# Two-chunk attention blocks from chunk 8 on, each behind an output projection

## The chip, the cores and the metric

One core of a Trainium2 chip runs the kernel. The metric is the time of one execution on the device, in microseconds, as the median of several runs. A profile of one execution gives the trace that is read below; engines are TensorE (PE, with its weight loads as PEld), VectorE (DVE), ScalarE (ACT), GpSimd (POOL) and SyncE (SP).

## What is computed

Sliding-window causal attention, then a SwiGLU feed-forward block on its output. Inputs are float32, and so is the output of 4608 x 512.

```
batch, n_heads, seq, head_dim = 8, 8, 576, 64;  window = 64
scores = (q @ k^T) / sqrt(64);  kept where 0 <= query - key < 64
attn_out = softmax(scores) @ v
x = attn_out.transpose(0, 2, 1, 3).reshape(4608, 512)
g = x @ w_gate                      # 512 x 1536
out = (g * sigmoid(g) * (x @ w_val)) @ w_out    # 1536 x 512
```

## The kernel before

The 4608 tokens are 36 chunks of 128. Four chunks make one FFN chunk c of 512 tokens (nine of them). All matmuls are bf16.

**Attention of a chunk n.** K and Q come from DRAM by DMAs that POOL issues (load, with a cast to bf16), then are transposed: chunks 0 to 9 two at a time by TensorE (T2, 16 transposes on tiles of 128x64, copied out by ACT), chunks 10 on by DMA transposes that SP issues in program order (T; Tkq is k and q). Scores are S(n) (Sa, Sb and the mask multiplication Sm on DVE) or, from chunk KC = 18 on, Sk(n), which lays keys out differently and has 16 matmuls where Sb has 24. Scores need the transposed k and q of their chunk and, in Sb, k of the chunk before, in Sk, q of the chunk after. ACT takes the exponentials into pt. The product with V is AVmm (32 matmuls on 64x64 tiles, in two phases), or AVs (16 matmuls on 128x64 tiles, for which vs holds V shifted by 64 rows; only chunks 0 to 3 use it). A column of ones in V yields the sums, and AVn (AVpn for two chunks) divides on DVE into xb. X(n) transposes xb into xT: by a DMA transpose on SP, or by four TensorE transposes with a copy on ACT or DVE.

**Blocks.** B(n) is AVmm phase 0 of chunk n, the scores of chunk n+1, AVmm phase 1, AVn. P(n) is the same for two chunks n and n+1: AVp phase 0, Sk(n+2), Sk(n+3), AVp phase 1, AVpn. P uses PSUM banks 0 to 6. B runs for chunks 4, 6 and 8 to 15, P from chunk P0 = 16 on.

**FFN.** F(c, fs, lo, hi) computes slices of 128 of the 1536 hidden columns for tokens lo to hi of chunk c: four matmuls for the gate, four for the value (per slice), tanh on ACT, two multiplications on DVE into hT. One slice on 512 tokens or two slices on 256 fill a PSUM bank each. O(c, u) is the output of 128 tokens: 12 matmuls over hT and Wo, a copy on ACT and a store.

**Order.** build() writes the whole order by hand up to chunk 11, and a loop over c = 2 to 8 and u = 0 to 3 the rest, with n = 4c + u + 4. Each operation goes to its engine's queue in that order; semaphores come from the reads and writes that an operation names. At most 16 DMAs of POOL, 16 of SP and 8 of ACT are under way. PSUM banks are taken from two lists, "f" for F, O and X, "a" for attention, which banks() replaces at given points. Buffers that a later load waits for: eight each for k and q of a chunk, ten for V.

Of the kernel before, what the change touches and what calls it, by code (L numbers as in the profile page):

```python
# [7 lines left out]
B, H, S, D = 8, 8, 576, 64  # L8
DM, DFF = H * D, 1536
T = B * S  # L10
NCH = T // 128
NFC = T // 512
NF = DFF // 128
# [139 lines left out]
class _Kernel:  # L153
# [7 lines left out]
    NO = 4  # L161
    NST = 4
    KC = 18
    P0 = 16

    def __init__(self, nc, q, k, v, wg, wv, wo, out):
        self.nc, self.q, self.k, self.v = nc, q, k, v
# [203 lines left out]
    def kt(self, n):  # L371
        return n + 3 + (n >= 13)

    def qt(self, n):
        return n + 3 + (n >= 12) + (n >= 15)
# [103 lines left out]
    def S(self, n, bias=False):  # L479
        if n < NCH:  # L480
            self.Sb(self.Sa(n, bias))
# [43 lines left out]
    def shift(self, n, r, eng):  # L525
        i = n + r - 1
        src, dst = self.va[n], self.vs[i]
        rows = slice(64 * r, 64 * r + 64)
        rd = [("va", n), ("va", n, 0), ("va", n, 1)] + (["mask"] if eng == "pool" else [])
        self.copy(eng, dst[rows, :, 0:64], src[rows, :, 0:64], rd, [("vs", i, r)])  # L530

    def AVs(self, st):
        n, bx, av, done = st
        va, pt = self.va[n], self.pt[n % self.NP]
        vs = self.vs[n - 1] if n else va

        def pe(e):
            for j in range(4):
                for p in range(2):
                    h = 2 * j + p  # L540
                    for c, vv in ((0, vs), (1, va)):
                        x = e.matmul(av[64 * c:64 * c + 64, p, j, :], pt[:, h, 64 * c:64 * c + 64], vv[:, h, 0:65],
                                     start=j == 0, stop=True, skip_group_check=True)
            return x

        ip = n % self.NP
        rd = [("pt", ip, 0), ("pt", ip, 1), ("va", n), ("va", n, 0), ("va", n, 1)]
        if n:
            rd += [("vs", n - 1, 0), ("vs", n - 1, 1)]
        done.append(self.g.op("pe", pe, reads=rd, writes=[b[1] for b in bx]))  # L550

    def AVn(self, st):
# [69 lines left out]
    def P(self, n):  # L622
        bx = [self.bank("a") for _ in range(3)]
        d = self.AVp(n, 0, bx, None)
        for m in (n + 2, n + 3):
            if m < NCH:
                self.Sk(m)
        self.AVp(n, 1, bx, d)
        self.AVpn(n, bx)

    def AV(self, n):
        st = self.AVa(n)
        self.AVmm(st, 0)
        self.AVmm(st, 1)
        self.AVn(st)
# [14 lines left out]
    def X(self, n, eng="sp", kind="f"):  # L650
        if n >= NCH:
            return
        g = self.g
        ix, it, u = n % 4, (n // 4) % self.NX, n % 4
        xb = self.xb[ix]
        xo = self.xT[it][:, :, 128 * u:128 * u + 128]
        xk = [("xb", ix, 0), ("xb", ix, 1)]
        if eng == "sp":
            g.op("sp", lambda e: e.dma_start_transpose(xo, xb[:, :]), reads=xk, writes=[("xT", it, u)], dma=True)
            return  # L660
        bank, bk = self.bank(kind)
        tb = bank[:, 0:256].bitcast(BF).rearrange("p (c t) -> p c t", c=4)

        def pe(e):
            for c in range(4):
                r = e.transpose(tb[:, c, :], xb[:, 128 * c:128 * c + 128], self.ident[:, :])
# [75 lines left out]
    def hTk(self, ih):  # L742
        return [("hT", ih, f) for f in range(NF)]

    def O(self, c, u):
        g = self.g
        ih = c % self.NH
        hT = self.hT[ih]
        io = (4 * c + u) % self.NO
        ost = self.ost[io]  # L750
        OB, ok = self.bank("f")

        def pe(e):
            for f in range(NF):
                r = e.matmul(OB[:, :], hT[:, f, 128 * u:128 * u + 128], self.Wo[:, f, :],  # L755
                             start=(f == 0), stop=(f == NF - 1))
            return r

        g.op("pe", pe, reads=self.hTk(ih) + [("Wo", f) for f in range(NF)], writes=[ok])
# [71 lines left out]
    def late_loads(self):  # L831
        self.load2(4, "k")
        self.load2(4, "q")
        self.load_wo(0, 6)
        self.load_wo(6, 12)
        self.load(10, "kq")
        self.load(8, "v")
        self.load(11, "kq")
        self.load(9, "v")

    def Tkq(self, n):
        self.T(n, "k")
        self.T(n, "q")

    def build(self):
        F, S, AV, X, T2, O = self.F, self.S, self.AV, self.X, self.T2, self.O
        self.loads()
        self.banks("a", [4, 5, 6, 7, 0, 1, 2, 3, 4, 5, 0, 1, 2, 3, 4, 5, 6, 7, 0, 1, 2, 3, 4, 5, 6, 7, 6, 7])
        self.warm(44, n=132)
        self.first_T(("dve", "act"))  # L850
        s0 = self.Sa(0)
        T2(0, "q", ("act", "dve"))
# [101 lines left out]
        lk, lq = 15, 15  # L954
        tk, tq = 14, 14
        for c in range(2, NFC):
            for u in range(4):
                n = 4 * c + u + 4
                if n == self.P0:
                    self.banks("f", [self.bank("f")[1][1], self.bank("f")[1][1], 5, 6, 7] + [7, 3, 4, 5, 6, 0, 1, 2, 7, 3, 4, 5, 6, 7] * 11)  # L960
                    self.banks("a", [0, 1, 2, 3, 4, 5, 6])
                if n == NCH:
                    self.banks("f", [3, 4, 5, 6, 0, 1, 2, 7])
                if n < NCH:
                    while lk < self.kt(n + 1):
                        lk += 1
                        self.load(lk, "k")
                    while lq < self.qt(n + 1):
# [3 lines left out]
                if n == 15:  # L972
                    self.init_kmask()
                if n < self.P0:
                    self.B(n)
                    self.X(n)
                if n < NCH:
                    while tk < self.kt(n):
                        tk += 1
                        self.T(tk, "k")  # L980
                    while tq < self.qt(n):
# [6 lines left out]
                if n == self.P0 - 1:  # L988
                    if n + 2 >= self.KC:
                        self.Sk(n + 2)  # L990
                        self.Sm(n + 2)
                    else:
                        S(n + 2)
# [5 lines left out]
                if self.P0 <= n < NCH - 2:  # L999
                    self.Sm(n + 2)  # L1000
                if n >= NCH and u == 3:
                    O(c - 1, u)
# [46 lines left out]
```

## Time and profile before

| | us |
|---|---|
| median of 3 runs | 331.41 |
| lowest, highest | 330.72, 331.79 |
| profiled execution | 330.58 |
| its span, first to last instruction | 328.8 |
| TensorE busy | 321.9 |
| VectorE busy | 202.0 |
| ScalarE busy | 136.8 |
| GpSimd busy | 107.0 |

In a row of the timeline stand the start, the time from the first start to the last end of merged instructions, engine and line, operation, tiles out<-in, the tile shape on the array, the shape of the data and the count; in brackets the idle time before and what ended it. Matmuls overlap, so that the next start tells more than the length. A row of one tile's instructions ends with their first and last start; "DMA to landing" is the time from the issue of a DMA to its last write. In a row of groups, busy time and mean ns follow the count. The clock granted to TensorE was 1.000 of full speed on average.

### The profile page before, as it was taken

The page shows a single profiled execution, that of the slowest core. Times are in us where ns is not written, and L with a number is a line of the kernel's source. Part 1 is how long each engine was busy: PE and PEld are TensorE (multiplying, and loading weights), DVE is VectorE, ACT ScalarE, POOL GpSimd, SP SyncE. Part 2 cuts the span into 40 slices and gives each one's busy share as a digit, 9 for nine tenths or more (in the row PEclk, how much of TensorE's full clock was granted, in tenths as well). Part 3 has the DMA queues.
Part 4 walks back from the last instruction along what each step waited for, and adds up shares of the span by engine and source line. Part 5 has one row for each costly group of instructions (what it writes and reads, how often), then busy time and mean ns, then how long its engine had stood idle before and what let it go on. Part 6 is the DMA issues. An engine that isn't in the chain of part 4 may idle for free.

```text
span 328.8 us, 8102 instructions
## 1 busy us (share of the span) xinstructions
PE 321.9 (98%) x3463; PEld 167.9 (51%) x3463; DVE 202.0 (61%) x350; ACT 136.8 (42%) x244; POOL 107.0 (33%) x137
## 2 busy tenths in 40 slices
PE   7999999999999999999999999999999999999997
PEld 6585576656444445454545454545454544444443
DVE  4676874675666657576666656565656566555520
ACT  2645665554334535252525252525243432332222
POOL 8999977544534444155151220100000000000000
PEclk9999999999999999999999999999999999999999
DMA  9999999999999999999999975562422111300012
GB/s 145 178 192 186 176 201 156 152 154 152 174 176 175 157 171 162 174 155 154 132 129 117 126 87 106 83 99 58 105 57 57 50 50 50 48 32 33 34 57 102
DMA packets 157892, 39.47 MB, mean 120 GB/s; under 512 B 144928, under 2 KB 153376, under 8 KB 157856
## 3 DMA queue, kind: packets, MB, share of 16 engines
q0 software_dynamic: 109008, 18.62, 74.6%
q1 hardware_dynamic: 43392, 10.82, 23.5%
q10 hardware_dynamic: 5456, 9.51, 8.9%
q8 instruction: 27, 0.44, 0.6%
q14 instruction: 9, 0.07, 0.1%
HBM read 37.75 MB, written 9.44 MB: 144 GB/s over the span
## 4 chain that ended last, share of the span: by engine, by line
PE 90%; POOL 4%; DMA 3%; ACT 1%; DVE 1%; issue 1%; ACTq 0%; POOLq 0%
PE ps L729 55%; PE ps L755 27%; DMA xT<-xb 3%; PE ps L590 2%; PE ps L514 1%; POOL va L314 1%; PE ps L457 1%; POOL vs L243 1%; PE ps L777 1%; PE ps L363 1%; POOL Wg L329 1%; POOL qs L323 1%; PE ps L421 0%; PE ps L425 0%; POOL Wv L329 0%
## 5 line engine op out<-in xcount | busy, mean ns | idle before, releaser
L737 DVE SCALAR_TENSOR_TENSOR uu<-sig,ps 128x512 bf16<-128x512 bf16 x108 | 73.9, 684 | 66.7 <-ACT sig L735 66.5
L729 PE MATMUL ps<-xT,Wg 128*128 128x512 bf16 (+1 forms) x480 | 111.3, 359 | 1.1 <-DMA xT<-xb 0.9
L729 PE MATMUL ps<-xT,Wv 128*128 128x512 bf16 (+1 forms) x480 | 111.1, 358 | 0.0
L755 PE MATMUL ps<-Wo,hT 128*128 128x512 bf16 x420 | 95.9, 380 | 0.0
L735 ACT ACTIVATE sig<-ps 128x512 bf16<-128x512 f32 x108 | 64.9, 600 | 70.9 <-PE ps L729 70.7
L739 DVE SCALAR_TENSOR_TENSOR hT<-uu,ps 128x512 bf16<-128x512 bf16 x108 | 74.2, 687 | 3.7
L729 PEld LDWEIGHTS ps<-xT,Wv 128*128 128x128 bf16 x480 | 46.9, 98 | 46.5
L729 PEld LDWEIGHTS ps<-xT,Wg 128*128 128x128 bf16 x480 | 44.5, 98 | 44.0 <-issue 1.6
L755 PEld LDWEIGHTS ps<-Wo,hT 128*128 128x128 bf16 x420 | 40.8, 98 | 49.0
L760 ACT ACTIVATE ost<-ps 128x512 f32<-128x512 f32 x35 | 20.9, 597 | 93.3 <-PE ps L755 93.3
L314 POOL DMA_DIRECT2D va<-in_v_dram x40 | 34.9, 883 | 32.6 <-PE ps L590 28.3
L314 POOL DMA_DIRECT2D kn<-in_k_dram x29 | 25.0, 867 | 36.6 <-DMA kT<-kn 29.6
L314 POOL DMA_DIRECT2D qn<-in_q_dram x29 | 24.9, 868 | 31.4 <-DMA qT<-qn 23.1
L433 ACT ACTIVATE pt<-ps 128x512 bf16<-128x512 f32 x36 | 19.4, 596 | 9.6 <-PE ps L425 9.2
L469 ACT ACTIVATE pt<-ps 128x512 bf16<-128x512 f32 x36 | 18.6, 603 | 3.7 <-PE ps L461 3.7
L617 DVE RECIPROCAL rp<-ps 128x14 f32<-128x14 f32 (+1 forms) x20 | 4.1, 204 | 25.6 <-PE ps L590 25.6
L477 DVE TENSOR_TENSOR pt<-pt,mask 128x1024 bf16<-128x1024 bf16 x14 | 9.6, 684 | 8.2 <-ACT pt L433 8.2
L619 DVE TENSOR_TENSOR xb<-ps,rp 128x896 bf16<-128x896 f32 (+1 forms) x20 | 13.8, 692 | 0.7
L477 DVE TENSOR_TENSOR pt<-pt,kmask 128x1024 bf16<-128x1024 bf16 x18 | 12.3, 685 | 0.0
L561 DVE TENSOR_TENSOR xb<-ps,rc 128x512 bf16<-128x512 f32 x16 | 11.1, 692 | 0.6
L590 PEld LDWEIGHTS ps<-va,pt 64*64 64x64 bf16 x632 | 7.7, 107 | 4.4 <-issue 4.2
L590 PE MATMUL ps<-va,pt 64*64 64x65 bf16 x632 | 9.5, 194 | 0.1
(64 smaller groups left out, 153.3 us busy)
## 6 DMA issues: line engine op xcount, KB each, us to landing
out_dram<-ost ACTq DMA_DIRECT2D x35, 256.0 KB, 3.3
va<-in_v_dram POOLq DMA_DIRECT2D x32, 128.0 KB, 10.8
kn<-in_k_dram POOLq DMA_DIRECT2D x23, 128.0 KB, 16.7
qn<-in_q_dram POOLq DMA_DIRECT2D x23, 128.0 KB, 16.6
Wg<-in_moe_w_gate_dram POOLq DMA_DIRECT2D x6, 256.0 KB, 7.4
Wv<-in_moe_w_val_dram POOLq DMA_DIRECT2D x6, 256.0 KB, 7.1
Wo<-in_moe_w_out_dram POOLq DMA_DIRECT2D x2, 768.0 KB, 14.5
qs<-in_q_dram POOLq DMA_DIRECT2D x3, 256.0 KB, 6.5
```

The costliest lines, as they stand in the source:

```text
L314: self.g.op("pool", lambda e, d=d, a=a: e.dma_start(d, a), writes=ks, dma=True)
L433: g.op("act", lambda e, po=po, p=p: e.activation(po, sv[p], ACTF.Exp, scale=SCALE), reads=[bx[p][1]], writes=[pk[p]])
L469: g.op("act", lambda e, po=po, p=p: e.activation(po, sv[p], ACTF.Exp, scale=SCALE), reads=[bx[p][1]], writes=[pk[p]])
L477: self.g.op("dve", lambda e: e.tensor_tensor(pt, pt, m, ALU.mult), reads=pk + [key], writes=pk)
L590: z = e.matmul(self.psa[64 * c:64 * c + 64, o:o + 65], pt[p][rows, h, 64 * a:64 * a + 64], va[m][rows, h, 0:65], start=first, stop=phase = ...
L619: g.op("dve", lambda e, d=d, num=num, rb=rb: e.tensor_tensor(d, num, rb, ALU.mult), reads=bk + [("rp", k)], writes=xk)
L729: r = e.matmul(bank[:, a * n:a * n + n], W[:, kk, f * 128:f * 128 + 128], xT[:, kk, lo:hi], start=(kk == 0), stop=(kk == NK - 1))
L735: g.op("act", lambda e, G=bank: e.activation(sig[:, 0:w], G[:, 0:w], ACTF.Tanh, scale=0.5), reads=[bk], writes=[("sig", i)])
L737: g.op("dve", lambda e: e.scalar_tensor_tensor(uu[:, 0:w], sig[:, 0:w], 1.0, G[:, 0:w], ALU.add, ALU.mult), reads=[("sig", i), gk], writes ...
L739: g.op("dve", lambda e: e.scalar_tensor_tensor(out, v3(uu), 0.5, v3(V), ALU.mult, ALU.mult), reads=[("uu", i), vk], writes=[("hT", ih, f) ...
L755: r = e.matmul(OB[:, :], hT[:, f, 128 * u:128 * u + 128], self.Wo[:, f, :], start=(f == 0), stop=(f == NF - 1))
L760: g.op("act", lambda e: e.activation(ost[:, :], OB[:, :], ACTF.Copy), reads=[ok], writes=[("ost", io)])
```

## The change

- Chunks 8 to 15 are done by P, two at a time, and no longer by B. P computes scores by Sb for chunks below 18. For n = 8 and 10 the second AV phase comes between the two scores. S(8) and S(9) run together ahead. Each of P(8), P(10), P(12), P(14) and P(16) follows an output O at once.
- AV of chunks 5 and 7 uses AVs; POOL makes the shifted copies in four more instructions, between loads (shift with a given buffer).
- FFN slices 6 and 7 of c = 1 are each done once on 512 tokens, not as a pair on two halves.
- x of chunk 10 is transposed by TensorE with a copy on ACT; that of chunk 7 is put between the halves of O(0,1) and copied by DVE.
- O(0,0) comes before AV of chunk 7, O(2,0) before c = 3, O(2,1) before P(16); the order of loads and transposes up to chunk 21 is written out, and the key mask is made earlier. P(16) and later blocks are as before.
- The warm-up matmuls are 48 of 121 columns, not 44 of 132.

```diff
+    def shift(self, n, r, eng, i=None):
+        i = n + r - 1 if i is None else i
...
     def AVs(self, st):
-        vs = self.vs[n - 1] if n else va
+        iv = n - 1 if n < 4 else (7 - n) // 2
+        vs = self.vs[iv] if n else va
...
     def P(self, n):
         for m in (n + 2, n + 3):
-            if m < NCH:
+            if m < self.KC:
+                self.Sb(self.Sa(m), False)
+            elif m < NCH:
                 self.Sk(m)
-        self.AVp(n, 1, bx, d)
+            if (m == n + 2) == (n < 12):
+                self.AVp(n, 1, bx, d)
         self.AVpn(n, bx)
...
-    def O(self, c, u):
+    def O(self, c, u, mid=None):
+        parts = ((0, NF),) if mid is None else ((0, NF // 2), (NF // 2, NF))
...
     def late_loads(self):
         self.load_wo(6, 12)
+        self.shift(4, 1, "pool", 1)
+        self.shift(5, 0, "pool", 1)
         self.load(10, "kq")
...
         self.load(9, "v")
+        self.shift(6, 1, "pool", 0)
+        self.shift(7, 0, "pool", 0)
...
-        self.warm(44, n=132)
+        self.warm(48, n=121)
...
-        AV(5)
+        a5 = self.AVa(5)
+        self.AVs(a5)
+        self.AVn(a5)
...
         F(1, (4, 5), 0, 256)
         X(6, "act")
         T2(4, "k", ("act", "act"))
-        F(1, (6, 7), 0, 256)
+        O(0, 0)
         a7 = self.AVa(7)
-        self.AVmm(a7, 0)
+        self.AVs(a7)
         T2(4, "q", ("act", "act"))
-        self.AVmm(a7, 1)
         self.AVn(a7)
         self.load(12, "kq")
         self.load(10, "v")
         for n in range(10, 12):
             self.Tkq(n)
-        O(0, 0)
-        X(7, "act")
+        O(0, 1, lambda: X(7, "dve"))
         self.load(13, "kq")
         self.load(11, "v")
         S(8)
-        O(0, 1)
+        S(9)
+        (new list of "f" banks)
+        F(1, (6,))
         self.load(14, "kq")
         self.load(12, "v")
         self.Tkq(12)
         F(1, (0, 1), 256, 512)
-        self.B(8)
-        X(8)
-        self.Tkq(13)
         F(1, (8,))
         self.load(15, "kq")
         self.load(13, "v")
+        self.Tkq(13)
         F(1, (2, 3), 256, 512)
-        self.B(9)
+        O(0, 2)
+        self.banks("a", [0, 1, 2, 3, 4, 5, 6])
+        self.P(8)
+        X(8)
         X(9)
         self.Tkq(14)
+        self.Sm(10)
         F(1, (9,))
+        self.Sm(11)
         F(1, (10,))
-        self.B(10)
-        O(0, 2)
         F(1, (4, 5), 256, 512)
-        X(10)
-        self.B(11)
+        O(0, 3)
+        self.P(10)
         F(1, (11,))
-        O(0, 3)
+        X(10, "act")
         X(11, "act")
-        F(1, (6, 7), 256, 512)
+        self.Sm(12)
+        F(1, (7,))
+        self.Sm(13)
+        self.load(16, "kq")
+        self.load(17, "k")
+        self.load(17, "q")
+        self.load(14, "v")
+        self.Tkq(15)
+        F(2, (0,))
+        F(2, (1,))
+        O(1, 0)
+        self.load(18, "kq")
+        self.load(15, "v")
+        self.Tkq(16)
+        F(2, (2,)); F(2, (3,)); F(2, (4,))
+        O(1, 1)
+        self.Tkq(17)
+        self.P(12)
+        self.load(19, "kq")
+        self.load(20, "q")
+        self.load(16, "v")
+        X(12); X(13)
+        self.Tkq(18)
+        F(2, (5,)); self.Sm(14); F(2, (6,)); self.Sm(15); F(2, (7,))
+        O(1, 2)
+        self.P(14)
+        self.load(20, "k")
+        self.load(21, "q")
+        self.load(17, "v")
+        X(14); X(15)
+        self.Tkq(19)
+        self.T(20, "q")
+        F(2, (8,)); self.Sm(16); self.init_kmask()
+        F(2, (9,)); self.Sm(17); F(2, (10,)); F(2, (11,))
+        O(1, 3)
+        O(2, 0)
...
-        for c in range(2, NFC):
+        for c in range(3, NFC):
...
                 F(c, (3 * u,))
                 F(c, (3 * u + 1,))
-                if n < NCH or u < 3:
+                if c == 3:
+                    if u != 1:
+                        O(2, max(u, 1))
+                elif n < NCH or u < 3:
                     O(c - 1, u)
-                if self.P0 <= n < NCH and u % 2 == 0:
+                if n < NCH and u % 2 == 0:
                     self.P(n)
                     X(n)
                     X(n + 1)
                 F(c, (3 * u + 2,))
```

More of the change, by code (lines that the diff above doesn't have):

```diff
@@ L548, in AVs @@
         if n:
-            rd += [("vs", n - 1, 0), ("vs", n - 1, 1)]
+            rd += [("vs", iv, 0), ("vs", iv, 1)]
         done.append(self.g.op("pe", pe, reads=rd, writes=[b[1] for b in bx]))
@@ L751, in O, with pe @@
         OB, ok = self.bank("f")
[L753 to L759, printed above, removed]
+        parts = ((0, NF),) if mid is None else ((0, NF // 2), (NF // 2, NF))
+        one = None
+        for a, b in parts:
+            def pe(e, a=a, b=b):
+                for f in range(a, b):
+                    r = e.matmul(OB[:, :], hT[:, f, 128 * u:128 * u + 128], self.Wo[:, f, :],
+                                 start=(f == 0), stop=(f == NF - 1), skip_group_check=mid is not None)
+                return r
+            one = g.op("pe", pe, reads=self.hTk(ih) + [("Wo", f) for f in range(NF)], writes=[ok], after=one)
+            if b < NF:
+                mid()
         g.op("act", lambda e: e.activation(ost[:, :], OB[:, :], ACTF.Copy), reads=[ok], writes=[("ost", io)])
@@ L927, in build @@
         S(8)
-        O(0, 1)
+        S(9)
+        x = self.bank("f")[1][1]
+        f = [(x + i) % 4 for i in range(4)]
+        self.banks("f", f + [4, f[0]] + [5, 6, 7, 7, 3, 4, 0, 5, 6, 7, 7, 3, 4, 5, 6, 0]
+                   + [1, 2, 3, 4, 5, 7, 0, 1, 2, 5, 6, 7, 7, 3, 4, 0, 5, 6, 7, 7, 3, 4, 5, 6, 0, 1, 2, 7, 3]
+                   + [1, 4, 5, 6, 7, 7, 3, 4, 5, 6, 0, 2, 7, 3, 4, 5, 6, 7] + [7, 3, 4, 5, 6, 0, 1, 2, 7, 3, 4, 5, 6, 7] * 10)
+        F(1, (6,))
         self.load(14, "kq")
@@ L938, in build @@
         self.load(13, "v")
+        self.Tkq(13)
         F(1, (2, 3), 256, 512)
-        self.B(9)
+        O(0, 2)
+        self.banks("a", [0, 1, 2, 3, 4, 5, 6])
+        self.P(8)
+        X(8)
         X(9)
         self.Tkq(14)
+        self.Sm(10)
         F(1, (9,))
+        self.Sm(11)
         F(1, (10,))
-        self.B(10)
-        O(0, 2)
         F(1, (4, 5), 256, 512)
-        X(10)
-        self.B(11)
+        O(0, 3)
+        self.P(10)
         F(1, (11,))
-        O(0, 3)
+        X(10, "act")
         X(11, "act")
-        F(1, (6, 7), 256, 512)
-        lk, lq = 15, 15
-        tk, tq = 14, 14
-        for c in range(2, NFC):
+        self.Sm(12)
[12 more added lines that the diff above has]
+        self.Tkq(16)
+        F(2, (2,))
+        F(2, (3,))
+        F(2, (4,))
+        O(1, 1)
[4 more added lines that the diff above has]
+        self.load(16, "v")
+        X(12)
+        X(13)
+        self.Tkq(18)
+        F(2, (5,))
+        self.Sm(14)
+        F(2, (6,))
+        self.Sm(15)
+        F(2, (7,))
+        O(1, 2)
[3 more added lines that the diff above has]
+        self.load(17, "v")
+        X(14)
+        X(15)
+        self.Tkq(19)
+        self.T(20, "q")
+        F(2, (8,))
+        self.Sm(16)
+        self.init_kmask()
+        F(2, (9,))
+        self.Sm(17)
+        F(2, (10,))
+        F(2, (11,))
+        O(1, 3)
+        O(2, 0)
+        lk, lq, tk, tq = 20, 21, 19, 20
+        for c in range(3, NFC):
             for u in range(4):
                 n = 4 * c + u + 4
-                if n == self.P0:
-                    self.banks("f", [self.bank("f")[1][1], self.bank("f")[1][1], 5, 6, 7] + [7, 3, 4, 5, 6, 0, 1, 2, 7, 3, 4, 5, 6, 7] * 11)
-                    self.banks("a", [0, 1, 2, 3, 4, 5, 6])
                 if n == NCH:
@@ L964, in build @@
                 if n < NCH:
-                    while lk < self.kt(n + 1):
+                    while lk < n + 5:
                         lk += 1
                         self.load(lk, "k")
-                    while lq < self.qt(n + 1):
+                    while lq < n + 6:
                         lq += 1
@@ L971, in build @@
                     self.load(n + 2, "v")
[L972 to L978, printed above, removed]
+                    while tk < n + 4:
                         tk += 1
                         self.T(tk, "k")
-                    while tq < self.qt(n):
+                    while tq < n + 5:
                         tq += 1
@@ L985, in build @@
                 F(c, (3 * u + 1,))
-                if n < NCH or u < 3:
+                if c == 3:
+                    if u != 1:
+                        O(2, max(u, 1))
+                elif n < NCH or u < 3:
                     O(c - 1, u)
[L988 to L993, printed above, removed]
-                if self.P0 <= n < NCH and u % 2 == 0:
+                if n < NCH and u % 2 == 0:
                     self.P(n)
@@ L998, in build @@
                 F(c, (3 * u + 2,))
-                if self.P0 <= n < NCH - 2:
+                if n < NCH - 2:
                     self.Sm(n + 2)
```

7 lines of the change are left out of this document (removed).

## The prediction

> **What bounds the kernel now.** I read the page first, then the list of waits on TensorE, then TensorE's timeline, and last the landings of single DMAs. The page's lines:
>
> ```profile
> span 328.8 us, 8102 instructions
> PE 321.9 (98%) x3463; PEld 167.9 (51%) x3463; DVE 202.0 (61%) x350; ACT 136.8 (42%) x244; POOL 107.0 (33%) x137
> DMA  9999999999999999999999975562422111300012
> ```
>
> TensorE (PE) is busy for 321.9 of 328.8 us; past the first 17 us I find two places where it stands for data, both taken up below. The DMA engines have work queued without a break up to slice 23, about 190 us. So the time is the length of TensorE's instruction stream, plus the places where that stream meets a DMA that lands late. An edit counts only if it shortens the stream or moves such a meeting. "Busy" doesn't give the stream's length, since matmuls overlap; the distance between starts does.
>
> ```profile
> 146.33 2.75 PE L755 MATMUL ps<-Wo,hT 128*128 128x512 bf16 x12
> 148.92 1.03 PE L729 MATMUL ps<-xT,Wg 128*128 128x512 bf16 x4
> 149.78 1.03 PE L729 MATMUL ps<-xT,Wv 128*128 128x512 bf16 x4
> ```
>
> By these starts an output O costs 148.92 - 146.33 = 2.59 us, half an FFN slice F on 512 tokens 0.865 us, a whole one 1.73.
>
> **Attention of chunks 8 to 15.** Before, each chunk has its own block B(n): half of the AV matmuls, the scores of the next chunk, the other half, all on 64x64 tiles between 128x128 work.
>
> ```profile
> 59.83 1.04 PE L729 MATMUL ps<-xT,Wv 128*128 128x256 bf16 x8
> 61.45 1.04 PE L729 MATMUL ps<-xT,Wg 128*128 128x512 bf16 x4
> ...
> 106.87 1.03 PE L729 MATMUL ps<-xT,Wv 128*128 128x512 bf16 x4
> 107.83 0.32 PE L514 MATMUL ps<-va,pt 64*64 64x65 bf16 x16
> 108.23 0.32 PE L514 MATMUL ps<-va,pt 64*64 64x65 bf16 x16
> 108.48 1.04 PE L729 MATMUL ps<-xT,Wg 128*128 128x512 bf16 x4
> ...
> 137.34 2.75 PE L755 MATMUL ps<-Wo,hT 128*128 128x512 bf16 x12
> 140.76 0.45 PE L590 MATMUL ps<-va,pt 64*64 64x65 bf16 x24
> 141.14 1.04 PE L729 MATMUL ps<-xT,Wg 128*128 128x512 bf16 x4
> ...
> 111.94 2.75 PE L755 MATMUL ps<-Wo,hT 128*128 128x512 bf16 x12
> 115.00 1.04 PE L729 MATMUL ps<-xT,Wg 128*128 128x512 bf16 x4
> ```
>
> The first and the last of the eight B's are here. The last takes 108.48 - 106.87 - 0.865 = 0.745 us; the first 61.45 - 59.83 - 0.87 = 0.75. About 0.1 us of it is the step into the small tiles (107.735 to 107.83). The block P for two chunks, used from chunk 16 on, takes 141.14 - 137.34 - 2.59 = 1.21 us, or 0.60 a chunk. Scores alone between large work cost 115.00 - 111.94 - 2.59 = 0.47 us (S(17); S(8), alone as well, is taken as equal). Inside a B, scores take about 0.25 us (the second AV half starts at 108.23, the first one's 16 matmuls ended about 107.98), so a visit to the small tiles costs 0.22 us by itself.
>
> Before: 8 x 0.745 + S(8) 0.47 + S(17) 0.47 = 6.90 us in ten visits. After: S(8) and S(9) together, 0.47 + 0.25 = 0.72, and four P's. No row shows a P with scores of the older form, which has 24 matmuls where P from 16 on has 16. I take 1.21 plus 2 x 0.015 for its 0.25 against 0.235 us per chunk, which gives 1.24; between 1.21 (as P now) and 1.49 (two B's). After: 0.72 + 4 x 1.24 = 5.68 us in five visits. **Gain 1.2 us**, 0.2 to 1.3 at the ends.
>
> One page of the Trainium skill speaks against this term. "TensorE: Matmul & The Clock Gate", section "Back-to-back issue gap", gives matmuls of up to 64 columns a floor of about 25 ns from start to start. By it the 24 matmuls of a chunk's scores would take 0.6 us. The row at 108.23 disagrees: two quarters of such matmuls go side by side here, 24 of them in 0.25 us, so the sum stays with the row. What the floor would do is the third rival.
>
> **AVs of chunks 5 and 7.** They get AVs, 16 matmuls of 128x64, where AVmm has 32 of 64x64.
>
> ```profile
> 37.21 0.64 PE L363 MATMUL ps<-ident,ks 128*64 128x128 bf16 x16
> 38.43 1.04 PE L729 MATMUL ps<-xT,Wg 128*128 128x512 bf16 x4
> ...
> 10.85 0.61 PE L363 MATMUL ps<-ident,qs 128*64 128x128 bf16 x16
> 11.30 0.42 PE L542 MATMUL ps<-va,pt 128*64 128x65 bf16 x16
> ...
> 16.22 0.19 PE L542 MATMUL ps<-vs,pt 128*64 128x65 bf16 x1 [0.20 <-POOL vs L243]
> 16.59 1.05 PE L729 MATMUL ps<-xT,Wg 128*128 128x256 bf16 x8
> ...
> 51.03 1.04 PE L729 MATMUL ps<-xT,Wv 128*128 128x256 bf16 x8
> 53.06 2.77 PE L755 MATMUL ps<-Wo,hT 128*128 128x512 bf16 x12
> ```
>
> Chunk 5 with the transposes (T2) ahead of it: 38.43 - 37.21 = 1.22 us now. T2 has the same tile shape as AVs, so there is no step between them: 0.45 (10.85 to 11.30) + 0.37 (16.22 to 16.59) = 0.82. Gain 0.40. Chunk 7: 53.06 - 51.03 - 0.87 = 1.16 now, three changes of tile around a T2. After: step in 0.1, AVs 0.26, T2 with its step out 0.57, that is 0.93. Gain 0.23. **Together 0.6 us.** The two slices on 512 tokens save 4 x 0.01 us, the warm-up has the same 5808 columns, and x of chunk 7 costs the same four transposes between two halves of an output. The key mask's three copies move on ACT, which is 42% busy. These are nothing.
>
> **x of chunk 10, and x of chunk 15.**
>
> ```profile
> 79.30 0.39 PE L666 MATMUL ps<-ident,xb 128*128 128x128 bf16 x4
> 79.52 1.04 PE L729 MATMUL ps<-xT,Wg 128*128 128x256 bf16 x8
> 80.39 1.04 PE L729 MATMUL ps<-xT,Wv 128*128 128x256 bf16 x8
> 82.93 1.02 PE L729 MATMUL ps<-xT,Wg 128*128 128x512 bf16 x4 [0.85 <-DMA xT<-xb]
> ...
> 115.88 1.03 PE L729 MATMUL ps<-xT,Wv 128*128 128x512 bf16 x4
> 117.12 1.02 PE L729 MATMUL ps<-xT,Wg 128*128 128x512 bf16 x4 [0.22 <-issue]
> ...
> L659 SPq DMA_TRANSPOSE xT<-xb x1: 1191/1191/1191, 110.1 to 110.1; - x1
> DMA to landing us min/median/max: 6.9/6.9/6.9
> ...
> 143.05 2.58 SPq L659 DMA_TRANSPOSE xT<-xb  x2
> ...
> DMA to landing us min/median/max: 7.3/9.0/9.1
> ```
>
> F(2,0) at 82.93 waits for the DMA transpose of chunk 10's x. 82.93 - 80.39 - 0.87 - 0.745 for B(12) leaves 0.92 us lost. The transpose on TensorE costs 79.52 - 79.30 = 0.22, so **0.7 us** is gained if nothing else is late there. Next late are x of chunks 8 and 9, still by DMA and now issued as a pair behind P(8). P(8) starts 14.2 us ahead of F(2,0) (P 1.24, F 3.46 + 1.75 + 1.73 + 1.73, O 2.59, P 1.24, two transposes 0.44). The pair of P(18), whose start is 137.34 + 2.59 = 139.9, was issued at 143.05 and 1.3 later, 3.1 and 4.4 us after it; the four x transposes of 63 to 84 us took up to 9.1 us to land (last row). 4.4 + 9.1 = 13.5 of 14.2 us, so it just holds.
>
> F(3,0) at 117.12 is labelled "issue", yet it starts 0.1 us after x of chunk 15 lands (110.13 + 6.9 = 117.03): 117.12 - 115.88 - 0.865 = **0.37 us**, a DMA wait too. After the change x of chunk 15 goes out behind P(14), and F(3,0) follows P(14)'s start by 1.24 + 6.92 + 5.18 = 13.3 us; issue at 4.4 and 6.9 to 9.0 us to land leave 2 us to nothing. It goes.
>
> **What it pays.**
>
> ```profile
> L243 POOL COPY vs<-va 64x512 bf16<-64x512 bf16 x5 | 3.1, 613 | 0.2
> ...
> L334 POOL DMA_DIRECT2D Wo<-in_moe_w_out_dram x2: 880/883/886, 32.9 to 33.8; - x2
> DMA to landing us min/median/max: 13.0/14.5/16.0
> ...
> L347 SPq DMA_TRANSPOSE qT<-qn x1: 1407/1407/1407, 130.4 to 130.4; - x1
> DMA to landing us min/median/max: 8.3/8.3/8.3
> ```
>
> O(0,0) moves ahead of AV 7. It needs all of Wo, whose second half lands at 33.8 + 16.0 = 49.8; TensorE would be there at 51.03 - 0.88 - 0.40 = 49.75. That costs nothing to 0.3 us; I take 0.1.
>
> The new copies into vs are four on POOL, 0.61 us each. POOL reaches the first two when it has issued Wo, about 34.7, and is done by 36; AVs(5) asks for them at about 37.7. Loads of chunks 10 and on are issued 1.2, then 2.5 us later, but they stand in one queue behind Wo, which takes 16.0 us to land, so their own landing doesn't move. If that queue were empty, the copies would cost those loads 2.5 us.
>
> P(18) is the dearer one. Its second scores, S(21), need q of chunk 22, transposed on SP behind x of chunks 16 and 17, which wait for P(16). That chain doesn't get shorter: issue at 130.4, landing at 130.4 + 8.3 = 138.7. S(21) now begins at 140.76 - 0.24 = 140.5, so it has 1.8 us to spare. After the change only one output lies between P(16) and P(18), not two (u = 1 of c = 3 has none, and O(2,1) is ahead of P(16)). S(21) comes 2.59 us earlier against its chain: 0.8 us late, plus 0.1 until TensorE moves. **0.9 us lost**; nothing if the transpose took 7.4 us, 1.5 if 8.9. Behind S(21) stand the rest of P(18) and all later TensorE work. Elsewhere the gap stays six slices and two outputs as now.
>
> Scores of chunks 13 to 17 come earlier, S(17) most of all: 104 for 114.5 (F(3,0) will be at 117.12 + 2.59 - 2.8 = 116.9, O(2,0) being ahead of it then, and P(14) 13.3 before). Their transposes lose what stood ahead of them on SP: x of 8 and 9 comes behind those of chunk 13, x of 12 and 13 behind those of chunk 17. Their loads on POOL keep the old order but for a few neighbours, and the buffers come free no later. I put nothing down for them.
>
> Sum: 1.2 + 0.6 + 0.7 + 0.4 - 0.1 - 0.9 = 1.9 us. The profiled execution took 330.58 (span 328.8 and 1.8 around it), so it would take 328.7; the median of the runs is 0.8 above it, 331.41 - 1.9 = **329.5 us**.
>
> **Rivals.** First, no new wait at P(18): the transposes land quicker since one x less is on the queue. Against it, the loads have not drained by 130 us (DMA row). It gives 2.8 us, 328.6. Chance 0.2.
>
> Second, the slower side: transposes on SP take longer by some L because they now come in pairs behind each P. It would be paid at F(2,0) (0.7 us of slack), F(3,0) (about 1.2) and S(21) (none). The forecast's gain is gone at L = 1.3 (0.6 + 0.1 + 1.3 = 2.0) and the kernel is slower by over 0.3% from L = 1.6 on (0.9 + 0.4 + 1.6 = 2.9); L = 2 costs 4.1, 333.6. For it: landings differ by 2.2 us already, 6.9 to 9.1. Against: one transpose less than now. Chance 0.1.
>
> Third, the change doesn't shorten the blocks: the older scores are paced by instruction, at T2's 0.45 / 16 = 28 ns. Sixteen more matmuls in each of four P's cost 1.8 us, S(9) 0.4: the first term turns to -1.0, the whole to a loss of 0.3, 331.7. The page's floor of 25 ns is an estimate of the same kind. Against it stands the row at 108.23. Chance 0.06. Small further waits of about a microsecond, at bank reuse or AVs, end within 0.3%: chance 0.08.
>
> **Numbers.** The forecast has the remaining 0.56. A measurement of this kernel tells 0.3%, 1 us, from no change. Faster by more: 0.56 less 0.03 for its upper edge, and 0.2, that is 0.73. Slower: 0.1 of the second rival and 0.01 of the third, 0.11. Same: the rest, 0.16. The range goes from the first rival less 0.4 for the spread of the runs and cheap P's, 328.2, up to a gain of only 0.3, 331.1: S(21) 0.6 dearer, 0.5 at F(2,0), 0.5 of spread.
>
> **What would show it.** In the changed profile: five attention visits between 55 and 106 us, P's of 1.24 us; F(3,0) at 116.9 and F(2,0) at 80.7 (36.2 ahead: twelve slices, five outputs, two P's), without idle; P(16) at 123.0 (3.46 + 2.59 later); a DMA wait of 0.9 us on TensorE at S(21), about 138. It is wrong if P(8) is near 1.5 us, if F(2,0) or F(3,0) still waits, or if some other transposed k or q shows up in TensorE's waits.

## The result, and the profile after

| | us |
|---|---|
| before, median of 12 runs (lowest to highest) | 331.60 (330.72 to 334.38) |
| after, median of 12 runs (lowest to highest) | 330.25 (329.41 to 331.49) |
| ratio after to before, 95% interval | 0.9952, 0.9929 to 0.9975 |
| profiled execution after | 329.87 |
| its span | 328.1 (before 328.8) |

In this series the changed kernel is faster by 0.25 to 0.7%; a second series, the control below, is less sure of it. The forecast was 329.5, with a range of 328.2 to 331.1. The line of the page after with the engines' busy time:

```profile
PE 321.3 (98%) x3423; PEld 167.1 (51%) x3423; DVE 202.5 (62%) x351; ACT 135.8 (41%) x244; POOL 109.3 (33%) x141
```

By the page almost nothing happened: TensorE's busy time fell by 0.6 us, the span by 0.7. The list of waits on TensorE (us in total, times, longest) tells more. The wait for x of chunk 10 (0.9 us) is not in it; three others are.

```profile
PE ps L756 <- DMA Wo<-in_moe_w_out_dram: 0.7, 1, 0.7
PE ps L450 <- issue: 0.5, 1, 0.5
PE ps L726 <- issue: 0.3, 1, 0.3
```

The first is O(0,0), the second S(21) in P(18), the third F(4,0). Now the gains, in TensorE's timeline. The AVs and O(0,0) come first, then S(8) and S(9), P(8), F(2,0), P(14) and F(3,0):

```profile
37.21 0.64 PE L362 MATMUL ps<-ident,ks 128*64 128x128 bf16 x16
38.03 1.04 PE L726 MATMUL ps<-xT,Wg 128*128 128x512 bf16 x4
...
49.19 0.64 PE L362 MATMUL ps<-ident,ks 128*64 128x128 bf16 x16
50.50 2.76 PE L756 MATMUL ps<-Wo,hT 128*128 128x512 bf16 x12 [0.68 <-DMA Wo<-in_moe_w_out_dram]
...
54.02 1.47 PE L756 MATMUL ps<-Wo,hT 128*128 128x512 bf16 x6
...
55.55 1.47 PE L756 MATMUL ps<-Wo,hT 128*128 128x512 bf16 x6
...
57.58 1.04 PE L726 MATMUL ps<-xT,Wg 128*128 128x512 bf16 x4
...
64.54 2.75 PE L756 MATMUL ps<-Wo,hT 128*128 128x512 bf16 x12
...
68.46 1.04 PE L726 MATMUL ps<-xT,Wg 128*128 128x512 bf16 x4
...
79.36 0.62 PE L663 MATMUL ps<-ident,xb 128*128 128x128 bf16 x8
79.81 1.03 PE L726 MATMUL ps<-xT,Wg 128*128 128x512 bf16 x4
...
81.54 1.03 PE L726 MATMUL ps<-xT,Wg 128*128 128x512 bf16 x4
...
101.82 2.75 PE L756 MATMUL ps<-Wo,hT 128*128 128x512 bf16 x12
...
105.69 1.04 PE L726 MATMUL ps<-xT,Wg 128*128 128x512 bf16 x4
...
112.60 5.34 PE L756 MATMUL ps<-Wo,hT 128*128 128x512 bf16 x24
117.78 1.03 PE L726 MATMUL ps<-xT,Wg 128*128 128x512 bf16 x4
```

- AV of chunk 5 with its T2 takes 38.03 - 37.21 = 0.82 us (1.22 before), AV of chunk 7 with its T2 54.02 - 50.50 - 2.59 = 0.93 (1.16 before).
- S(8) with S(9): 57.58 - 55.55 - 1.30 (half an output) = 0.73. P(8): 68.46 - 64.54 - 2.59 = 1.33. P(14): 105.69 - 101.82 - 2.59 = 1.28. In the same way P(10) takes 1.36 and P(12) 1.28, so that these visits take 5.98 us together, against 6.90 before.
- F(2,0) at 81.54 follows the start of the slice before it (79.81) by 1.73, one slice's time, so without a wait; the eight transposes for x of 10 and 11 take 0.45. F(3,0) at 117.78 follows two outputs by 5.18: no wait either.

Against that, O(0,0) starts 1.31 us behind its T2 at 49.19, which had 0.57 before. The last rows are those of P(18) and F(4,0):

```profile
135.48 2.75 PE L756 MATMUL ps<-Wo,hT 128*128 128x512 bf16 x12
...
139.34 0.24 PE L450 MATMUL ps<-qT,kT 64*64 64x128 bf16 x2 [0.48 <-issue]
...
139.97 1.04 PE L726 MATMUL ps<-xT,Wg 128*128 128x512 bf16 x4
...
148.62 1.03 PE L726 MATMUL ps<-xT,Wv 128*128 128x512 bf16 x4
149.92 1.02 PE L726 MATMUL ps<-xT,Wg 128*128 128x512 bf16 x4 [0.28 <-issue]
```

P(18) takes 139.97 - 135.48 - 2.59 = 1.90 us, 0.70 more than the 1.20 that it takes without a wait (1.21 before the change). F(4,0) comes 1.30 behind the start of the last half slice, 0.44 more than without a wait. Both are put down to "issue"; the landings name the transfer. The rows are the two Wo loads, the transpose of q of chunk 22, and those of x of chunks 18 and 19:

```profile
L333 POOL DMA_DIRECT2D Wo<-in_moe_w_out_dram x2: 880/883/886, 32.9 to 33.8; - x2
DMA to landing us min/median/max: 13.7/15.2/16.7
...
L346 SPq DMA_TRANSPOSE qT<-qn x1: 1576/1576/1576, 131.1 to 131.1; - x1
DMA to landing us min/median/max: 8.2/8.2/8.2
...
L656 SPq DMA_TRANSPOSE xT<-xb x2: 1196/1596/1997, 141.9 to 143.1; - x2
DMA to landing us min/median/max: 6.2/6.4/6.7
```

Wo is there at 33.8 + 16.7 = 50.5, q of 22 at 131.1 + 8.2 = 139.3, x of 19 at 143.1 + 6.7 = 149.8: each about 0.1 us or less ahead of the instruction that waited. Before the change, F(4,0) and the transposes for x of 18 and 19 stood so:

```profile
150.65 1.03 PE L729 MATMUL ps<-xT,Wg 128*128 128x512 bf16 x4
...
L659 SPq DMA_TRANSPOSE xT<-xb x2: 1192/1270/1348, 143.0 to 144.3; - x2
DMA to landing us min/median/max: 5.8/6.2/6.5
```

x of 19 landed at 144.3 + 5.8 = 150.1, half a microsecond ahead of F(4,0). So the account is: 0.40 + 0.23 (AVs) + 0.92 (attention) + 0.70 (x of 10) + 0.37 (x of 15) - 0.74 (Wo) = 1.88 us gained by F(3,0), where the rows give 117.12 + 2.59 - 117.78 = 1.93; then 0.70 at S(21), 0.44 at F(4,0) and 0.06 in P(16) are paid, and 0.73 us is left, the difference of the spans.

### The profile page after: what moved, and what is told of

Its sections match the earlier page's. It is cut to its first block, busy times and chain, and to the rows that moved or that the text cites. A ratio compares the mean times of both kernels' runs of the same rounds, so it can differ in the third digit from the quotient of the medians.

```text
span 328.1 us, 8030 instructions
## 1 busy us (share of the span) xinstructions
PE 321.3 (98%) x3423; PEld 167.1 (51%) x3423; DVE 202.5 (62%) x351; ACT 135.8 (41%) x244; POOL 109.3 (33%) x141
## 4 chain that ended last, share of the span: by engine, by line
PE 88%; POOL 5%; DMA 5%; issue 1%; DVE 0%; POOLq 0%
PE ps L726 53%; PE ps L756 28%; DMA Wo<-in_moe_w_out_dram 5%; PE ps L584 3%; PE ps L450 1%; POOL va L313 1%; POOL qs L322 1%; POOL vs L242 1%; PE ps L780 1%; POOL ks L322 1%; POOL Wg L328 1%; PE ps L414 1%; POOL Wv L328 0%; PE ps L362 0%; PE ps L663 0%
## 5 line engine op out<-in xcount | busy, mean ns | idle before, releaser
L726 PEld LDWEIGHTS ps<-xT,Wv 128*128 128x128 bf16 x472 | 46.2, 98 | 47.2
L611 DVE RECIPROCAL rp<-ps 128x14 f32<-128x14 f32 (+1 forms) x28 | 5.7, 204 | 34.5 <-PE ps L584 34.5
L613 DVE TENSOR_TENSOR xb<-ps,rp 128x896 bf16<-128x896 f32 (+1 forms) x28 | 19.4, 692 | 1.0
L584 PEld LDWEIGHTS ps<-va,pt 64*64 64x64 bf16 x888 | 10.8, 107 | 6.1 <-issue 5.5
L584 PE MATMUL ps<-va,pt 64*64 64x65 bf16 x888 | 13.4, 194 | 0.1
L418 PE MATMUL ps<-qT,kT 64*64 64x64 bf16 x288 | 7.6, 194 | 0.2 <-issue 0.2
```

Source lines behind the costliest of these rows:

```text
L584: z = e.matmul(self.psa[64 * c:64 * c + 64, o:o + 65], pt[p][rows, h, 64 * a:64 * a + 64], va[m][rows, h, 0:65], start=first, stop=phase = ...
L613: g.op("dve", lambda e, d=d, num=num, rb=rb: e.tensor_tensor(d, num, rb, ALU.mult), reads=bk + [("rp", k)], writes=xk)
L726: r = e.matmul(bank[:, a * n:a * n + n], W[:, kk, f * 128:f * 128 + 128], xT[:, kk, lo:hi], start=(kk == 0), stop=(kk == NK - 1))
```

## Experiments

Theory A for the waits: each hangs on TensorE's own work (a place in an order, a cover between two blocks), so it goes when that is changed. Theory B: the DMA engines work off a backlog at their own pace, so time won earlier on TensorE is met again at the next landing. Ratios are to the kernel before, from the same series of runs.

**The changed kernel again, as a control.** No edit.

> The changed kernel once more, beside the three variants of it. 1.0 to 2.0 us faster than before by the medians. Its trace again: O(0,0) waits 0.4 to 1 us for Wo, S(21) in P(18) about 0.7 us for q of chunk 22, F(4,0) 0.2 to 0.7 us for x of chunk 19. If one of these is absent in this second profile, it was chance and not the schedule.

Measured: 330.62 us (328.76 to 332.96), ratio 0.9987 (0.9961 to 1.0013), span 328.4. The three waits stand in the same places:

```profile
50.46 0.82 PE L756 MATMUL ps<-Wo,hT 128*128 128x512 bf16 x3 [0.61 <-DMA Wo<-in_moe_w_out_dram]
...
139.57 0.24 PE L450 MATMUL ps<-qT,kT 64*64 64x128 bf16 x2 [0.71 <-issue]
...
150.26 1.02 PE L726 MATMUL ps<-xT,Wg 128*128 128x512 bf16 x4 [0.39 <-issue]
```

The places are stable, but by the ratio the gain in this series is 0.4 us where the first had 1.6 (0.6 and 1.35 by the medians), and its interval includes no change. The two intervals overlap; neither series alone fixes what the change is worth.

**q of chunk 22 ahead of P(16).** It no longer stands behind x of 16 and 17 on SP.

```diff
-                    while tk < n + 4:
+                    while tk < n + 4 + (n == 16):
...
-                    while tq < n + 5:
+                    while tq < n + 5 + (n == 16):
```

> k of chunk 21 and q of chunk 22 are transposed on SP ahead of P(16), not behind x of chunks 16 and 17. Both theories: the wait of 0.7 us inside P(18) goes, P(18) takes 1.2 us for 1.9. Theory A (each wait hangs on TensorE's own work ahead of it): the whole 0.7 us stays gained, the wait at F(4,0) stays 0.4 us. Theory B (DMA landings up to about 150 us come off a backlog with its own pace, and what is gained earlier is met again at the next operation that needs a DMA): F(4,0) still starts at about 149.5 to 149.9, its wait grows to about 1.0 us, and the end moves by 0.2 us at most.

Measured: 328.55 us (328.07 to 331.43), ratio 0.9929 (0.9905 to 0.9953), span 326.4. P(18) and F(4,0):

```profile
134.90 2.75 PE L756 MATMUL ps<-Wo,hT 128*128 128x512 bf16 x12
...
138.69 1.04 PE L726 MATMUL ps<-xT,Wg 128*128 128x512 bf16 x4
...
147.34 1.03 PE L726 MATMUL ps<-xT,Wv 128*128 128x512 bf16 x4
148.20 1.03 PE L726 MATMUL ps<-xT,Wg 128*128 128x512 bf16 x4
```

P(18) takes 1.20 us, as before the change: the wait at S(21) is gone, and it did hang on the place in the order. F(4,0) does not wait at all, which neither theory had; x of 18 and 19 land in 4.3 to 5.1 us here. This version is faster than the changed kernel, whose interval in the same series does not reach 0.9953. Part of the 2.0 us of span between them is luck of the execution, though: it has no Wo wait, without an edit there. The step also moves loads: POOL issues three of them sooner, at 129.2 to 130.9 us, so that only four go out from 137 to 144 us, where the changed kernel has seven from 138 to 144.

**Work put between T2 and O(0,0).** Slices 6 and 7 of c = 1 are done in halves again, and the first half stands where O(0,0) stood (the bank list is changed to suit).

```diff
         T2(4, "k", ("act", "act"))
-        O(0, 0)
+        F(1, (6, 7), 0, 256)
...
-        O(0, 1, lambda: X(7, "dve"))
+        O(0, 0, lambda: X(7, "dve"))
...
-        F(1, (6,))
+        O(0, 1)
...
-        F(1, (7,))
+        F(1, (6, 7), 256, 512)
```

> FFN slices 6 and 7 of c = 1 are done in two halves of 256 tokens again, and their first half stands between the transposes of chunk 8 and AV 7, so that O(0,0) comes 2 to 3 us later, behind AV 7. Both: no wait for Wo at O(0,0), 0.04 us for the halves, P(8) to P(16) 0.7 us earlier. Theory A: S(21) and F(4,0) keep their waits of 0.7 and 0.4, the end is 0.7 us earlier. Theory B: S(21) keeps 0.7, since its chain starts at P(16), but F(4,0) waits about 1.0, and the end moves by 0.2 us at most.

Measured: 329.86 us (328.79 to 330.61), ratio 0.9947 (0.9918 to 0.9975), span 327.9. The Wo wait is gone, and P(16) comes 0.43 us earlier, at 123.49 for 123.92. But S(21) waits as long, and F(4,0) waits 0.72 (149.75 - 148.17 - 0.865) where it waited 0.44:

```profile
138.89 0.24 PE L450 MATMUL ps<-qT,kT 64*64 64x128 bf16 x2 [0.47 <-issue]
...
148.17 1.03 PE L726 MATMUL ps<-xT,Wv 128*128 128x512 bf16 x4
149.75 1.02 PE L726 MATMUL ps<-xT,Wg 128*128 128x512 bf16 x4 [0.56 <-issue]
```

F(4,0) is 0.17 us earlier than in the changed kernel, although P(16) was 0.43 earlier: most is given back in this execution, as theory B says. The medians don't show it: 329.86 is 0.76 below the control of the same series, where theory B had 0.2 at most, but the two intervals overlap.

**Both, and x of 18 and 19 by TensorE.**

```diff
                 F(c, (3 * u,))
+                if n == 19:
+                    X(18, "act")
+                    X(19, "act")
                 F(c, (3 * u + 1,))
```

(with the two edits above, without the DMA transposes of 18 and 19, and the bank list lengthened to suit)

> Both edits above, and x of chunks 18 and 19 transposed by TensorE (0.44 us) with copies on ACT, so that F(4,0) needs no DMA. 0.75 - 0.04 + 0.7 + 0.44 - 0.44 = 1.4 us less than the changed kernel by both theories, about 327 span. By theory B this is far more than the two edits bring one by one (0.2 each at most), by theory A it is their sum.

Measured: 328.75 us (328.62 to 329.14), ratio 0.9927 (0.9899 to 0.9955), span 326.8, with no wait over 0.2 us behind the first 17 us. It is no faster than the one-line edit alone, but its runs lie within 0.5 us. Both theories had this sum, so it does not tell them apart.

**The AVs of 5 and 7 alone, in the kernel before.** Only AVs for these two chunks and the four copies on POOL.

```diff
...
-        AV(5)
+        a5 = self.AVa(5)
+        self.AVs(a5)
+        self.AVn(a5)
...
-        self.AVmm(a7, 0)
+        self.AVs(a7)
         T2(4, "q", ("act", "act"))
-        self.AVmm(a7, 1)
```

> The kernel before with one part of the change alone: AVs for chunks 5 and 7. TensorE's stream is 0.63 us shorter. If gains add up, the end comes 0.6 us earlier. If TensorE is held by DMAs: x of chunk 10 is issued on SP behind q of chunk 14, which waits for a load that lands at 72.5 whatever TensorE does, so F(2,0) still starts at about 82.9, its wait grows from 0.9 to 1.5 us, and the end moves by less than 0.2 us.

Measured: 332.07 us (330.09 to 333.92), ratio 1.0014 (0.999 to 1.0038), span 329.1.

```profile
83.33 0.81 PE L730 MATMUL ps<-xT,Wg 128*128 128x512 bf16 x3 [1.52 <-DMA xT<-xb]
...
L660 SPq DMA_TRANSPOSE xT<-xb x1: 1363/1363/1363, 73.9 to 73.9; - x1
DMA to landing us min/median/max: 9.1/9.1/9.1
```

The wait for x of chunk 10 grows: its transpose lands at 83.0, no earlier than before (73.7 + 9.1 = 82.8), and the 0.63 us won at the AVs is gone by F(2,0). (One matmul record of that slice is missing, so it starts about 0.22 ahead of the row; by the starts the wait is 1.46 us for 0.92 before. The rest was lost ahead of it, 0.25 us in a pause inside B(9) whose cause the trace doesn't name.) The POOL copies are not what held the transpose: they put the loads back by 2.4 us at 46 us, but by 0.3 at 50 us, and the transpose of x of 10 by 0.2. Alone this part is worth nothing; with x of 10 on TensorE it counts in full by the account above. This is theory B at its clearest.

**x of chunk 10 by TensorE alone, in the kernel before.**

```diff
-        X(10)
+        X(10, "act")
```

> The kernel before with x of chunk 10 transposed by TensorE and copied by ACT, nothing else. F(2,0) 0.7 us earlier and without a wait. If gains add up (x of chunk 15 hangs on B(15), that is on TensorE), F(3,0) keeps its 0.37 us and the end is 0.7 us earlier. If DMAs hold TensorE later on, F(3,0) waits about 1 us and the end moves by 0.2 us at most.

Measured: 330.06 us (329.81 to 334.21), ratio 0.9967 (0.9941 to 0.9992), about 1.1 us faster for one word, more than the 0.7 of the better case. The profiled execution was the slowest, 334.21: its granted clock fell to 0.87 between 10 and 20 us and it is 3.6 us late from there on, so its starts are not compared one to one. F(2,0) waits for nothing in it, while F(3,0) waits about 1 us for x of chunk 15 (0.37 before) and, less the offset, starts where it did. Whether a gain is given back there at the full clock, this trace can't show.

**Two outputs between P(16) and P(18) again.** O(2,0) and O(2,1) where the kernel before had them.

```diff
         O(1, 3)
-        O(2, 0)
...
-                if c == 3:
-                    if u != 1:
-                        O(2, max(u, 1))
-                elif n < NCH or u < 3:
+                if n < NCH or u < 3:
```

> The changed kernel with O(2,0) and O(2,1) back where the kernel before had them (behind F(3,1) and in u = 1 of c = 3), so that two outputs lie between P(16) and P(18) again. Theory A (S(21) waits because one output less covers the chain P(16), x of 16 and 17, transpose of q of 22): the 0.70 us at S(21) goes, with about 1.9 us to spare; but F(3,0) is reached 2.59 us earlier, at 115.2, and x of chunk 15 lands at about 116.5, so a wait of about 1.3 us appears there. F(4,0) keeps its 0.4. Sum: 0.6 us slower than the changed kernel, span about 328.7, ratio to the kernel before 0.997. Theory B (the transposes go at the pace of the loads' backlog, whatever TensorE does): the same at S(21) and F(3,0), but F(4,0), reached 0.6 later, waits no longer: within 0.2 us of the changed kernel.

Measured: 330.34 us (329.68 to 333.63), ratio 0.9969 (0.9941 to 0.9996), span 327.9.

```profile
112.17 2.75 PE L756 MATMUL ps<-Wo,hT 128*128 128x512 bf16 x12
116.28 1.02 PE L726 MATMUL ps<-xT,Wg 128*128 128x512 bf16 x4 [1.35 <-DMA xT<-xb]
```

S(21) doesn't wait (P(18) takes 1.20 us), so the missing output is why it did. F(3,0) waits 116.28 - 112.17 - 2.59 = 1.52 us, 0.2 more than expected, F(4,0) not at all, and the span is that of the changed kernel within 0.2. That is theory B's figure: what the two later waits cost, 0.70 and 0.44, was paid at F(3,0) instead. The rest of the 1.52 has its match in O(0,0), which waited for Wo 0.3 us here and 0.74 there.

**Less load.** Two kernels leave V loads out (the blocks then use older rows of V); TensorE's work is unchanged. First the loads of chunks 26 and 27 only, which are issued with x of 18 and 19:

```diff
             src = {"k": self.k, "q": self.q, "v": self.v}[x]
+            if x == "v" and 26 <= n < 28:
+                continue
             if x == "v":
```

> The changed kernel without the loads of V of chunks 26 and 27 (their buffers keep older values, so that part of the attention is not computed from its V). Seven loads go out together at 138 to 144 us, when k of chunk 21 has been transposed, and x of chunks 18 and 19 is transposed among them. If that burst makes F(4,0) wait, x of 19 lands 1 us earlier and F(4,0) waits for nothing, while the 0.7 us in P(18) stay; span 0.4 less. If F(4,0) waits only because P(18) was held up, its 0.4 us stay.

Measured, one run: 328.64 us, span 326.9.

```profile
138.64 0.24 PE L452 MATMUL ps<-qT,kT 64*64 64x128 bf16 x2 [0.51 <-issue]
...
147.92 1.03 PE L728 MATMUL ps<-xT,Wv 128*128 128x512 bf16 x4
148.78 1.03 PE L728 MATMUL ps<-xT,Wg 128*128 128x512 bf16 x4
```

S(21) waits as ever, F(4,0) no longer (148.78 - 147.92 = 0.86). Then the loads of chunks 18 to 24, which are on their way while q of 22 is transposed:

```diff
+            if x == "v" and 18 <= n < 25:
+                continue
```

> The changed kernel without the V loads of chunks 18 to 24 (these blocks use older rows of V, so the output is another there): seven loads of POOL less between about 115 and 150 us, TensorE's work the same. Theory A (the transpose of q of 22 takes 8.2 us because loads share the DMA engines with it): it lands in 5 to 7 us, and S(21) waits at most 0.2 us, not 0.70; F(4,0) does not wait either; span 327.0. Theory B (the transpose is late by its place in SP's order, behind x of 16 and 17, and takes 7 to 8 us anyway): S(21) keeps a wait of 0.5 us or more, span 327.5 or more.

Measured, one run: 328.43 us, span 326.3, neither wait, and by chance none for Wo. That closes the account: 328.1 - 0.74 - 0.70 - 0.44 = 326.2. The transpose of q of 22 is issued at the same time as in the changed kernel, 131.1:

```profile
L348 SPq DMA_TRANSPOSE qT<-qn x1: 1213/1213/1213, 131.1 to 131.1; - x1
DMA to landing us min/median/max: 2.5/2.5/2.5
```

It lands in 2.5 us and not in 8.2 (5 to 7 were expected), so 5.7 us of the 8.2 is the V loads' doing. The Trainium skill says, in "DMA: Bandwidth & Descriptors", section "Issuing engines are not separate DMA queues", that DMAs started by ScalarE, SyncE and GpSimd run on the same 16 engines and interleave; POOL's loads and SP's transposes here agree with it.

**The early transpose with other company.** With both edits of before (early and cover), and with the early step kept from n = 16 on (`n >= 16` for `n == 16`):

> The changed kernel with k of 21 and q of 22 transposed ahead of P(16), and with slices 6 and 7 of c = 1 in halves so that O(0,0) comes behind AV 7; x of 18 and 19 stay on DMA. No wait on TensorE between 20 and 330 us over 0.2 us; span 326.2 to 326.7; 2.3 to 2.9 us faster than before. If the landing of Wo had nothing to do with the spread, it is as fast as the early transposes alone.

> The changed kernel with the transposes of k and q from n = 16 on put one chunk earlier for good, not only once (at P(16) those of k of 21 and q of 22, at n = 17 k of 22 and q of 23, and so on). Theory A (q of 22 must not stand behind x of 16 and 17; one step is enough, and the rest changes nothing): no wait at S(21), as with the single step, 2.0 us less span than the changed kernel's 328.1 to 328.4, 326.4; ratio to the kernel before 0.993. Theory B (k of 22 and later now stand ahead of x of each pair on the queue of SP, and the x transposes land later by about a microsecond): S(21) does not wait, but F(4,0) waits 0.5 us or more, span about 327.3, ratio 0.995.

Measured: early and cover 329.55 us (328.75 to 331.88), ratio 0.9949 (0.9932 to 0.9966), span 327.3; one ahead for good 329.46 (328.96 to 329.91), ratio 0.9939 (0.9918 to 0.996), span 327.4. S(21) waits in neither. F(4,0) waits in both, by the starts 149.24 - 147.30 - 0.865 = 1.07 us and 149.26 - 147.51 - 0.865 = 0.89 us:

```profile
149.24 1.02 PE L726 MATMUL ps<-xT,Wg 128*128 128x512 bf16 x4 [0.91 <-DMA xT<-xb]
```

```profile
149.26 1.02 PE L726 MATMUL ps<-xT,Wg 128*128 128x512 bf16 x4 [0.72 <-DVE uu L734]
```

(In the second row the label names VectorE, but x of 19, issued at 142.0, lands 7.2 us later at 149.2.) For the first I had expected no wait. For the second, theory B's figures came, but the first has the same wait without that theory's cause. Three kernels with x of 18 and 19 on DMA now share the early transpose, and one of them, in its profile, has no wait at F(4,0). The number of loads from 137 to 144 us does not sort them: four where there is no wait, four and eight where there is one. What does differ is how far the loads lag. These are the rows of the K load that each issues at about 137 us, for the early transpose alone and then with the cover:

```profile
L313 POOL DMA_DIRECT2D kn<-in_k_dram x1: 881/881/881, 137.3 to 137.3; - x1
DMA to landing us min/median/max: 5.0/5.0/5.0
```

```profile
L313 POOL DMA_DIRECT2D kn<-in_k_dram x1: 878/878/878, 137.0 to 137.0; - x1
DMA to landing us min/median/max: 8.6/8.6/8.6
```

It is 8.4 in the third. The lag of 5.0 goes with no wait, 8.4 and 8.6 with 0.9 and 1.1 us; that the lag is the cause is not shown. Why it is shorter in one execution than in another, with the same loads in the same order in the first two, stays open; the runs were on different chips, and I did not separate that from the edits.

Taken together, the traces of the AVs alone, of the cover and of the two outputs show theory B's figures. With the early transpose alone neither theory's came, and x of chunk 10 alone and the kernel with everything do not tell the two apart.

## Why the prediction was right, and where it was off

**The result.** 329.5 was forecast, 1.9 us faster; the first series gave 330.25, the second 330.62. Direction and range held, but the range was wide: it held any gain from 0.3 to 3.2 us. For the profiled execution the sum gave 328.7, and 329.87 was measured. Term by term, the attention gave 0.28 us less, Wo cost 0.64 more, S(21) 0.20 less, and 0.44 at F(4,0) and 0.06 in P(16) were not in the sum. The error at S(21) was luck, since it hid part of the others.

**TensorE's stream: right.** The AVs were put at 0.63 and gave 0.63, the swap of x of 10 at 0.7 and gave 0.70, x of 15 at 0.37 and gave it. F(2,0) and F(3,0) came without idle time and 36.2 us apart, as forecast, but at 81.54 for 80.7 and 117.78 for 116.9, mostly for Wo. That a gain counts only where it moves a meeting with a DMA was borne out more strongly than I had put it: the AVs alone gave nothing.

**The attention blocks: right in kind, mis-sized.** P was taken at 1.24 and measured 1.28 to 1.36, so the term is 0.92, not 1.2. Both P's in which the second AV phase comes between the two scores (1.33, 1.36) are dearer than those in which it follows them (1.28, 1.28). There is one more change of operation inside, which may be why; no run tries the other order. The third rival, a pace of 28 ns for each added score matmul, would have made a P 1.7 us long and is refuted. P(8) has 64 matmuls for AV and 48 for the scores, 112 of 64 to 128 columns in 1.33 us, 12 ns each. The Trainium skill gives a floor of about 25 ns for matmuls of up to 64 columns ("TensorE: Matmul & The Clock Gate", section "Back-to-back issue gap"). By these 12 ns the floor does not hold for a stream of matmuls on tiles of 64x64.

**Wo: the largest mis-sized term in this profile.** I put 0.1 us on O(0,0), between nothing and 0.3, from one landing at 49.8. The landing was 50.5, and 0.74 was lost. At the full clock the second half of Wo landed between 49.7 and 50.7 in the profiles with a record of it, while TensorE is there at 49.75, so this wait varies from execution to execution. Seven profiles are of kernels that are the same up to there: the changed kernel twice, the early transpose, one ahead, the outputs back, and the two with less load. O(0,0) waits 0.7 us in the first two and 0 to 0.3 in the other five. So the size forecast was the common one, and the row was wrongly read as a fixed number: behind this backlog the landing has a spread of about a microsecond.

**S(21): right.** 0.9 us was forecast for the step behind one output less, with q of 22 named; 0.70 was measured, with 8.2 us for the transpose where 8.3 was taken. TensorE and the transpose both came 0.6 to 0.7 us later than forecast, so that the difference held. The runs show each link: with the transpose put early it goes, with the output put back it goes, with fewer loads it goes.

**F(4,0): missed.** "Elsewhere the gap stays six slices and two outputs as now" was true of TensorE's work and wrong as an argument. TensorE reaches F(4,0) at 148.62 + 0.865 = 149.49, 1.16 us earlier than before (150.65), while x of 19 lands at 149.8, only 0.3 earlier than the 150.1 of before. The slack was 0.5 us, and the prediction did not look at it. A gap that stays the same is not enough when the transfer in it goes at the pace of the loads around it: seven loads are issued in the 6 us around those two transposes, and without two of them the wait is gone (one run). The sign "if some other transposed k or q shows up" looked for the wrong tensor: it was an x.

**The rivals.** The first, no new wait at P(18), did not come about. The second, longer transposes, was not seen at F(2,0) and F(3,0), where it was looked for; a small form of it had its part at F(4,0): x of 19 took 6.7 us for 5.8 before.

## What to carry to other kernels

Where an engine that is 98% busy meets transfers that land from a backlog, list the slack at every such meeting, not only at the places that wait now: time won upstream is paid at the first one whose landing does not move. Take a landing time behind a backlog as a number with a spread (here about 1 us) when something is moved up to it. And look for the step that stands in the wrong place of an in-order queue: one transpose issued a block earlier took away the 0.70 us at S(21), three quarters of what the rebuilt attention of eight chunks gained, though in two of three kernels F(4,0) took about 0.4 us of it back.

## What was not expected of the hardware

A DMA transpose that took 2.5 us took 8.2 us when seven more loads of another engine's queue were under way, at the same time of issue (131.1 us). Loads issued in the same order at nearly the same time lagged 5.0 us in one execution and 8.6 in another. One execution had a granted clock of 0.87 from 10 to 20 us and was 3.6 us late from about there on.
